# Late attention sums and some turns in two 64-row halves of the array, with four PSUM banks shared and a new order of steps

## The chip, the cores and the metric

The kernel runs on one core of a Trainium2 chip. The metric is the device time of one execution in microseconds (us), before and after one change.

## What is computed

The reference is linear attention followed by a highway layer. For 8 batches (b) and 8 heads, with 576 positions and 64 features a head:

```python
q_s = softmax(q, axis=-1);  k_s = softmax(k, axis=2)      # over features; over positions
kv  = einsum('bhsd,bhse->bhde', k_s, v)                    # 64 x 64 for each head
x   = einsum('bhsd,bhde->bhse', q_s, kv)                   # then 4608 rows of 512
H = max(x @ w_h, 0);  T = sigmoid(x @ w_t + b_t)
out = T * H + (1 - T) * x                                  # 4608 x 512, float32
```

## The kernel before

The 4608 rows are 36 tiles of 128 rows. Tiles 9p to 9p+3 belong to batch 2p, 9p+4 to 9p+7 to batch 2p+1, and 9p+8 takes 64 rows of each ("double tile"). All engines work at once. Their order is written out by hand: `ORDER` is one long list of steps, such as `xu_9_0` or `th_9_0:A`, and each step issues its instructions to its engine in the order of the list. What follows the colon chooses the engine (A ScalarE, D VectorE, P GpSimd) or a form. Every engine works off its own instructions in that order and waits only for data and free buffers. The engines are named as in the profile: PE is TensorE (PEld its weight loads), DVE is VectorE, ACT is ScalarE, POOL is GpSimd, SP is SyncE, which issues nearly all transfers.

The steps of one batch b:

- `k`, `v`, `q` (L180, L193): loads, three landing buffers each, all from SP's queue; the stores `st` (L473) stand in the same queue. For batch 7 `qd` (L337) turns the queries by two DMA transposes, from the same queue.
- `ek`, `eq` (L250, L294): exponentials on ACT. `vc` (L256): cast of v to fp16, by default on POOL.
- `kv` (L262): the products of k and v, 72 matmuls of 64 rows x 64 columns for a batch (two steps of 36 for batches 0 and 1), which use the array in four quarters. `kr` (L278): reciprocal; `kn` (L283): the product with it. `kn` writes the result into `kvb`, a matrix that is zero outside two blocks, so that one matmul over 128 rows makes two heads; it takes two instructions, one for each half of the partitions.
- `qt` (L310): eight (or two) TensorE turns of the query exponentials into the bank `qps`; `qc` (L329) copies them out.

The steps of one tile i:

- `xu` (L348): the sums, four matmuls of 130 columns; 65 columns a head, one of them the sum of the softmax. A double tile has eight, on the two column halves of the array (form `128*64` in the profile). `rs` (L367): reciprocal; `x` (L372): product, both on DVE.
- `xt` (L379): four TensorE turns of x into the bank `turned`; `xe` (L387): copy out, on DVE or ACT.
- `bw` (L394): the bias into a bank `tps`, by a matmul or by an ACT copy (:A). `mt` (L406): four matmuls of 512 columns with w_t onto it. `mh` (L414): four with w_h into a bank `gps`. Tiles 0, 4 and 5 do most steps in two halves.
- `th` (L428): tanh on ACT. `dd` (L437) on DVE. `uu` (L441): the gate, one DVE instruction, or, with :P, two on POOL (a "lifted" gate: L450 and L451). `oo` (L462): the last addition, on POOL. `st`: the store.

`fill` (L165) are matmuls without use before the first loads have landed. The last tile, 35, does its gate in two column halves.

PSUM has eight banks: two for `tps`, two for `gps`, two for the one pair `ps_x` that `kv` and `xu` use in turn, one for `qps`, one for `turned` (L97 to L101, L115).

Of the kernel before, what the change touches and what calls it, by code (L numbers as in the profile page):

```python
# [18 lines left out]
w_t_2 kr_0_0 whd_0:P whd_2:P w_t_0 k_1_2 v_1_2 q_1_0 k_1_0 v_1_0 fill_5 q_1_4 kn_0_0 q_2_0 k_2_0 eq_0_2 xu_0_0 v_2_0  # L19
q_3_0 rs_0_0 whc_0:A x_0_0 k_3_0 fill_4 v_3_0 kv_0_1 fill_3 kr_0_1 kn_0_1 xu_0_1 rs_0_1 xu_1_0 rs_1_0 qt_0_1 x_1_0  # L20
fill_6 whd_3:P qc_0_1 xt_1_0 xu_3_0 qt_0_2 qc_0_2:A xe_1_0:D fill_1 rs_3_0 x_3_0 x_0_1 xt_3_0 xu_2_0 rs_2_0 x_2_0
wtc_2:P whc_2:A mh_1_0 wtc_0:P vc_1_3 ek_1_3 ek_1_2 vc_1_0 xe_3_0:D mh_3_0 dd_1 xt_0_1 xt_0_0 mt_1_0 xe_0_0:D mh_0_0
xe_0_1 dd_3 xt_2_0 mh_0_1 mt_0_1 th_1_0 xe_2_0:D dd_0 vc_1_2:A kv_1_1 uu_1_0 oo_1_0 eq_1_0 mt_0_0 th_0_0 ek_1_0 ek_1_1
kr_1_1 bw_3 qt_1_0 vc_1_1:A kn_1_1 qc_1_0 mt_3_0 xu_5_1 uu_0_0 mh_2_0 th_3_0 bw_2 rs_5_1 x_5_1 dd_2 xu_4_1 kv_1_0
kr_1_0 eq_1_1 rs_4_1 xt_5_1 mt_2_0 th_2_0 kn_1_0 bw_5 xe_5_1:D x_4_1 xu_5_0 mt_5_1 qt_1_1 eq_1_2 rs_5_0 x_5_0 xt_5_0
xu_4_0 bw_4:A uu_3_0:P oo_3_0 xe_5_0:D mh_5_1 rs_4_0 x_4_0 mh_5_0 xt_4_1 qc_1_1:A xt_4_0 xe_4_1:D dd_5 eq_2_0 xe_4_0:D
v_4_0 mt_5_0 th_5_0 xu_6_0 qt_1_2 rs_6_0 qc_1_2 oo_0_0 mt_4_1 mh_4_1 mh_4_0 uu_2_0:P x_6_0 mt_4_0 eq_2_1 xt_6_0 xu_8_0
uu_5_0 bw_6:A xe_6_0:D qt_2_0 rs_8_0 x_8_0 mh_6_0 oo_5_0 th_4_0 xt_8_0 dd_4 uu_4_0 xu_7_0 mt_6_0 ek_2_0:F rs_7_0
vc_2_2:A bw_8 xe_8_0:D mt_8_0 x_7_0 th_6_0 xt_7_0 th_8_0 oo_2_0 vc_2_0 kv_2_0 oo_4_0 qc_2_0 q_4_0 bw_7:A qt_2_1
qc_2_1:A dd_6 uu_6_0:P oo_6_0 eq_3_0:F xe_7_0:D kr_2_0 kn_2_0 mh_8_0 xu_9_0 rs_9_0 x_9_0 mt_7_0 th_7_0 bw_9 dd_8  # L30
uu_8_0:P qt_2_2 qc_2_2:A xu_10_0 bw_10:A xt_9_0 xe_9_0:D rs_10_0 x_10_0 ek_3_0 mh_7_0 dd_7 ek_3_2 mh_9_0 xu_12_0 k_4_0
xt_10_0 k_5_0 rs_12_0 qt_3_0 xe_10_0:D x_12_0 mt_9_0 th_9_0 uu_7_0:P q_4_9 dd_9 xu_11_0 qc_3_0 vc_3_2:A xt_12_0
mt_10_0 rs_11_0 mh_10_0 x_11_0 v_5_0 q_5_0 vc_3_0 st_1_1 q_5_9 uu_9_0 dd_10 oo_7_0 kv_3_0 qt_3_1 th_10_0 oo_8_0 st_1_0
xe_12_0 bw_12:A mh_12_0 kr_3_0 qc_3_1:A kn_3_0 xu_14_0 rs_14_0 x_14_0 bw_11:A xt_11_0 xe_11_0 mt_12_0 th_12_0 qt_3_2
v_6_0 xt_14_0 oo_9_0 k_6_0 xu_13_0 q_6_0 xe_14_0 mh_11_0 dd_12 qc_3_2 mt_11_0 rs_13_0 eq_4_0:F th_11_0 uu_12_0
uu_10_0:P x_13_0 dd_11 xu_15_0 rs_15_0 vc_4_0 mh_14_0 x_15_0 st_5_1 dd_14 qt_4_0 oo_10_0 vc_4_2 xu_16_0 rs_16_0 x_16_0
xt_13_0 xe_13_0:D oo_12_0 bw_14:A bw_13:A ek_4_0:F st_3_0 mt_14_0 th_14_0 xu_17_0 rs_17_0 bw_15:A x_17_0 qc_4_0
xt_15_0 mt_13_0 kv_4_0 xe_15_0:D kr_4_0 uu_11_0:P oo_11_0 th_13_0 qt_4_1 uu_14_0:P st_3_1 mh_13_0 vc_5_2 xt_16_0
kn_4_0 mh_15_0 xe_16_0:D vc_5_0 xu_18_0 ek_5_0:F dd_13 xt_17_0 qc_4_1:A uu_13_0 xe_17_0:D dd_15 rs_18_0 oo_14_0
bw_16:A mt_15_0 mh_16_0 x_18_0 th_15_0 uu_15_0:P mt_16_0 dd_16 mh_17_0 oo_13_0 bw_17:A th_16_0 oo_15_0 kv_5_0 uu_16_0  # L40
kr_5_0 kn_5_0 oo_16_0 eq_4_2 dd_17 qt_4_2 xt_18_0 eq_5_0 mt_17_0 st_5_0 xe_18_0 xu_20_0 rs_20_0 mh_18_0 qc_4_2:A
bw_18:A q_7_0 th_17_0 mt_18_0 eq_5_1 bw_20:A uu_17_0:P x_20_0 xt_20_0 dd_18 vc_6_2 xe_20_0:D xu_21_0 th_18_0 rs_21_0
# [23 lines left out]
def kernel(  # L66
# [40 lines left out]
    b32 = consts.tile([P, DM], FP32, name="b32")  # L107
# [28 lines left out]
    def halves(b, k):  # L136
        return (k, k + 1) if b < 2 else (0, 2)
# [396 lines left out]
```

## Time and profile before

| what | value |
|---|---|
| device time, median of 3 runs | 118.9 us (118.82 to 118.92) |
| the profiled execution, first to last instruction (span) | 116.9 us |
| what lies around the span, by the median | 2.0 us |
| mean granted TensorE clock | 0.995 |
| moved by DMA | 40.58 MB, mean 347 GB/s |
| first matmul of the highway layer (`mh_1`) | 18.14 us |

The profiled execution has no time of its own besides its span; the runs differ among themselves by 0.1 us.

How to read the rows quoted below. A window row gives a stretch, its length, then the busy time of each engine with its count of instructions, the granted clock, the share of the DMA engines and what they moved. A timeline row gives the start, the length, the engine, the line, the operation, what it writes and reads with its shape, and how many instructions are merged in it; brackets tell of idle time before it and what ended it. A matmul's form such as `64*64` is the part of the array that it uses, rows by columns. The length of a matmul holds its way through the array, so neighbours overlap, and the distance from one start to the next is its cost. A group row ends with total busy time, mean ns of one, and idle time before it with its cause.

### The profile page before, as it was taken

The page shows a single profiled execution, that of the slowest core. Times are in us where ns is not written, and L with a number is a line of the kernel's source. Part 1 is how long each engine was busy: PE and PEld are TensorE (multiplying, and loading weights), DVE is VectorE, ACT ScalarE, POOL GpSimd, SP SyncE. Part 2 cuts the span into 40 slices and gives each one's busy share as a digit, 9 for nine tenths or more (in the row PEclk, how much of TensorE's full clock was granted, in tenths as well). Part 3 has the DMA queues.
Part 4 walks back from the last instruction along what each step waited for, and adds up shares of the span by engine and source line. Part 5 has one row for each costly group of instructions (what it writes and reads, how often), then busy time and mean ns, then how long its engine had stood idle before and what let it go on. Part 6 is the DMA issues. An engine that isn't in the chain of part 4 may idle for free.

```text
span 116.9 us, 3424 instructions
## 1 busy us (share of the span) xinstructions
PE 109.5 (94%) x1351; PEld 61.6 (53%) x1351; DVE 93.3 (80%) x222; ACT 90.0 (77%) x132; POOL 89.1 (76%) x99
## 2 busy tenths in 40 slices
PE   5999987999999999999999999999999999999930
PEld 2354544545665656565665547566564555554520
DVE  5642587589799979979889798988989887899870
ACT  4356461897999999989999999998597998545520
POOL 5022237208996999999999999999989699999960
PEclk9999999999999999999999999999999999999998
DMA  2999999999999999999999999999999956992875
GB/s 42 399 392 377 408 398 385 375 377 379 393 391 397 383 391 393 358 375 387 357 376 360 387 392 363 390 381 383 399 398 217 302 204 270 397 404 115 315 295 179
DMA packets 24195, 40.58 MB, mean 347 GB/s; under 512 B 5362, under 2 KB 11762, under 8 KB 24180
## 3 DMA queue, kind: packets, MB, share of 16 engines
q1 hardware_dynamic: 24032, 40.24, 96.9%
q8 instruction: 10, 0.16, 0.6%
q10 hardware_dynamic: 148, 0.14, 0.4%
q14 instruction: 5, 0.04, 0.1%
HBM read 30.41 MB, written 9.44 MB: 341 GB/s over the span
## 4 chain that ended last, share of the span: by engine, by line
PE 67%; POOL 15%; issue 6%; DVE 5%; DMA 3%; SPq 1%; POOLq 0%; DVEq 0%
PE tps L411 18%; PE gps L419 16%; PE turned L167 9%; POOL o L471 7%; PE xu L361 6%; PE turned L384 5%; PE kv L269 5%; PE qps L324 4%; POOL u L451 4%; DMA out_dram<-o 3%; POOL g L450 2%; PE qps L319 2%; POOL v L259 2%; DVE x L376 2%; PE tps L401 1%
## 5 line engine op out<-in xcount | busy, mean ns | idle before, releaser
L471 POOL TENSOR_TENSOR o<-u,x 128x512 f32<-128x512 f16 (+1 forms) x36 | 40.6, 1143 | 1.6 <-DVE u L453 0.7
L411 PE MATMUL tps<-w16t,xT 128*128 128x512 f16 (+1 forms) x148 | 37.3, 373 | 0.0
L419 PE MATMUL gps<-w16h,xT 128*128 128x512 f16 x144 | 36.8, 379 | 0.5 <-DVE xT L391 0.5
L376 DVE TENSOR_TENSOR x<-xu,rs 128x512 f16<-128x512 f32 (+1 forms) x39 | 25.2, 649 | 2.4
L259 POOL CAST v<-v 128x1152 f16<-128x1152 f32 (+1 forms) x14 | 14.0, 1010 | 14.7 <-DMA v<-in_v_dram 13.7
L439 DVE SCALAR_TENSOR_TENSOR d<-x,gps 128x512 f16<-128x512 f16 x36 | 24.5, 680 | 0.3
L451 POOL TENSOR_TENSOR u<-g,d 128x512 f16<-128x512 f16 x17 | 19.7, 1158 | 1.7 <-DVE rs L370 0.4
L253 ACT ACTIVATE ek<-k 128x576 f16<-128x576 f32 (+2 forms) x15 | 17.9, 1225 | 3.0 <-DMA k<-in_k_dram 3.0
L419 PEld LDWEIGHTS <-xT 128*128 128x128 f16 x144 | 13.0, 98 | 12.3 <-DVE xT L391 1.8
L399 ACT COPY tps<-ball 128x512 f32<-128x512 f32 x28 | 16.6, 597 | 3.5 <-DVE u L453 3.2
L411 PEld LDWEIGHTS <-xT 128*128 128x128 f16 x148 | 13.2, 98 | 10.6 <-DVE xT L391 0.4
L361 PE MATMUL xu<-kvb,eq 128*128 128x130 f16 (+1 forms) x160 | 14.8, 224 | 0.2 <-DVE kvb L287 0.2
L384 PE MATMUL turned<-idh,x 128*128 128x128 f16 x144 | 14.2, 220 | 0.5 <-DVE x L376 0.5
L391 DVE COPY xT<-turned 128x512 f16<-128x512 f16 (+1 forms) x28 | 10.9, 391 | 4.2 <-PE turned L384 3.0
L435 ACT ACTIVATE tps<-tps 128x512 f32<-128x512 f32 (+1 forms) x20 | 11.2, 559 | 3.6 <-PE tps L411 3.3
L453 DVE SCALAR_TENSOR_TENSOR u<-tps,d 128x512 f16<-128x512 f32 (+1 forms) x19 | 12.7, 671 | 1.4 <-ACT tps L435 0.6
L361 PEld LDWEIGHTS <-eq 128*128 128x128 f16 (+1 forms) x160 | 10.0, 100 | 7.3 <-DVE x L376 2.5
L167 PE MATMUL turned<-blank 128*128 128x512 f16 x40 | 12.4, 458 | 1.5 <-POOL blank L149 1.3
L384 PEld LDWEIGHTS <-x 128*128 128x128 f16 x144 | 9.8, 98 | 6.0 <-DVE x L376 2.1
L307 ACT ACTIVATE qe<-q 128x1024 f16<-128x1024 f32 (+3 forms) x9 | 9.4, 1052 | 4.1 <-DMA q<-in_q_dram 4.1
L450 POOL TENSOR_SCALAR g<-th 128x512 f16<-128x512 f16 x17 | 10.6, 621 | 0.9 <-ACT th L433 0.9
L433 ACT ACTIVATE th<-tps 128x512 f16<-128x512 f32 x17 | 10.0, 594 | 0.9 <-PE tps L411 0.9
(48 smaller groups left out, 106.8 us busy)
## 6 DMA issues: line engine op xcount, KB each, us to landing
k<-in_k_dram SPq DMA_DIRECT2D x6, 1152.0 KB, 12.2
v<-in_v_dram SPq DMA_DIRECT2D x6, 1152.0 KB, 12.0
out_dram<-o SPq DMA_DIRECT2D x23, 256.0 KB, 4.0
q<-in_q_dram SPq DMA_DIRECT2D x10, 512.0 KB, 11.5
out_dram<-o SPq DMA_DIRECT2D x6, 512.0 KB, 3.8
k<-in_k_dram SPq DMA_DIRECT2D x4, 576.0 KB, 9.3
q<-in_q_dram SPq DMA_DIRECT2D x2, 1152.0 KB, 14.2
q<-in_q_dram SPq DMA_DIRECT2D x2, 640.0 KB, 10.5
```

What stands on the lines that cost most here:

```text
L167: nc.tensor.matmul(spare, blank[:, 0:P], blank, start=True, stop=True, skip_group_check=True)
L253: nc.scalar.activation(t[:, :, c:c + n].rearrange("p j c d -> p c j d"), T[f"k32{b}"][:, c:c + n].rearrange("p c (j d) -> p c j d", j=NJ), ...
L259: copy(v16[b % NV][:, c:c + n, :, 0:D], T[f"v32{b}"][:, c:c + n].rearrange("p c (j d) -> p c j d", j=NJ))
L361: nc.tensor.matmul(dst, turned_q(b, jp, n), kvb[b % NKV][:, hh, kk], start=True, stop=True, skip_group_check=True)
L376: nc.vector.tensor_mul(t[:, k0:k1], sums(i, k)[:, :, :, 0:64], T[f"rs{i}_{k}"][:, 0:k1 - k0].unsqueeze(3).to_broadcast([P, k1 - k0, 4, D]))
L384: nc.tensor.matmul(t[:, n], T[f"x{i}"][:, n0 + n % 2:n0 + 2 * P:2], idh, is_transpose=True, start=True, stop=True, skip_group_check=True)
L399: nc.scalar.copy(t[:, cs], ball[:, cs])
L411: nc.tensor.matmul(T[gate(i, k)][:, cs], T[f"xT{i}"][:, n], w16["t"][:, n, cs], start=False, stop=(n == parts[-1] and not first), skip_gro ...
L419: nc.tensor.matmul(t, T[f"xT{i}"][:, n], w16["h"][:, n], start=(first and n == parts[0]), stop=(n == parts[-1] and not (first and len(part ...
L439: nc.vector.scalar_tensor_tensor(t, T[f"x{i}"], -0.5, T[f"gps{i}"], op0=ALU.mult, op1=ALU.max)
L451: nc.gpsimd.tensor_mul(t, g, T[f"d{i}"])
L471: eng.tensor_add(t[:, cs], T[f"u{i}_{h}"][:, cs], T[f"x{i}"][:, cs])
```

## The change

1. **Sums from tile 9 on in halves of 64 rows.** A new matrix `kvl` holds the key-value product of both heads without zeros, with ones at its edges (`setuplate`, three small POOL memsets early on). `xu` issues eight matmuls of 64 rows and 65 columns in place of four of 128 rows and 130 columns; the two halves write two banks. Double tiles 17, 26 and 35 issue sixteen, in quarters.
2. **The key-value norm of batches 2 to 7 in one instruction**, since `kvl` has no blocks to keep apart.
3. **Turns in halves.** From tile 9 and batch 3 on, a turn that is not marked `:W` in the list is made of 64-row halves into two banks, twice as many matmuls of 64 columns. These are `xt` of tiles 17, 20, 21, 24, 25, 26, 28, 29, 31, 32, 33 and 34 and `qt` 5_0, 6_0 and 6_1; the other 25 late turns are marked `:W`. `xe` and `qc` read the two banks in one instruction.
4. **Four banks given out one by one.** The pair `ps_x` and the banks `qps` and `turned` become two pairs, `ps_s`; `pair_user` and the loop behind it go through the list and give each use a pair, or a bank to a turn marked `:W`. Early turns and fills share one pair.
5. **The bias on DVE** (`bw:D`) is a new choice.
6. **A new list** with the same steps and `setuplate`. Counts of what changes its engine:

| step | before | after |
|---|---|---|
| `bw` | 9 PE, 28 ACT | 5 PE, 22 ACT, 10 DVE (2, 3, 7, 10, 15, 18, 23, 24, 25, 28) |
| `uu`, by tile | 19 DVE, 17 POOL | 15 DVE, 21 POOL |
| `vc`, batches 2 to 7 | 10 POOL, 2 ACT | 6 POOL, 6 ACT |
| `vc`, batches 0 and 1 | 4 POOL, 3 ACT, 1 DVE | 3 POOL, 4 ACT, 1 DVE |
| `qc`, wide (g 0 and 1) | 8 DVE, 6 ACT | 12 DVE, 2 ACT |
| `qc`, narrow (g 2) | 2 DVE, 6 ACT | 6 DVE, 2 ACT |
| `xe` | 28 DVE, 11 ACT | 27 DVE, 12 ACT |
| `wtc` | 2 POOL | 1 POOL, 1 ACT |

The TensorE steps of the new list from the first late sum on; a bar stands where the division of the array changes (52 here, 13 ahead of it). In the old list it changes only into and out of its ten `kv` steps and its four double sums, which all stand alone (28).

```
xu_11 xu_10 | mt_6 mt_4_1 mt_4 xt_10 qt_3_1 mh_4_1 xt_11 mh_10 | xu_9 xu_12 | mt_11 mt_10 qt_3_0 qt_3_2 xt_9 mh_11
xt_12 | kv_3 | mt_9 | xu_13 xu_14 | mh_9 mh_12 xt_14 mt_12 | xu_16 xu_15 | mh_14 mt_14 xt_13 xt_16 qt_4_1 mh_13 xt_15
mt_13 qt_4_0 mh_16 | kv_4 xu_17 | mt_15 mt_16 | xu_21 xt_17 | mh_15 | qt_5_0 xt_21 | mt_17 | xu_20 xu_18 | mh_17 mh_21
mt_21 | xt_20 | kv_5 | xu_19 | mh_20 qt_4_2 xt_18 mt_20 xt_19 qt_5_1 mt_18 | xu_23 xu_24 | mh_19 mh_18 | xu_22 xt_24 |
mt_19 xt_23 qt_5_2 mt_24 xt_22 | xu_26 | mh_24 mt_23 | qt_6_0 xu_25 | mh_22 mt_22 | xt_26 xt_25 | mh_23 | qt_6_1 | kv_6 |
mh_25 | xu_27 xu_29 | mh_26 mt_25 xt_27 mt_26 | xu_28 xt_29 | mh_27 mh_29 | kv_7 | xt_28 | mt_27 | xu_33 xu_32 | mh_28
mt_28 | xt_32 xt_33 | mt_29 | xu_34 xu_31 | mh_33 mh_32 mt_32 | xt_31 xu_30 | mt_33 qt_6_2 qt_7_2 mh_31 xt_30 mt_31 |
xu_35 | xt_34 | mt_30 mh_30 mh_34 xt_35 mt_34 bw_35_1 bw_35_0 mh_35 mt_35 mt_35_1
```

SP's queue around the last loads, before: `q_7_0 st_7_0 v_7_0 st_7_1 st_10_1 k_7_0 st_10_0 qd_7_0 q_7_9 qd_7_1`; after: `q_7_0 st_7_0 k_7_0 v_7_0 st_12_0 st_16_0 st_10_0 qd_7_0 qd_7_1`. Nine stores stand ahead of the last large load in both.

The core of the diff (the lists are left out):

```diff
-    ps_x = pool("ps_x", 1, space=PS)
-    ps_q = pool("ps_q", 1, space=PS)
-    ps_xt = pool("ps_xt", 1, space=PS)
+    ps_s = pool("ps_s", 1, space=PS)
...
+    EARLY, EARLY_Q = 9, 3
...
+    banks = [ps_s.tile([P, 2, DM], FP32, tag=f"s{i}", name=f"space{i}") for i in range(2)]
+    space, held = {}, [None] * 4
+    for now, (u, s) in enumerate(zip(users, ORDER.split())):
+        if u and u not in space:
+            last = [-1 if h is None else final[h] for h in held]
+            if s.endswith(":W"):
+                n = min((n for n in range(4) if last[n] < now), key=lambda n: (last[n ^ 1] < now, last[n]))
+                space[u], held[n] = banks[n // 2][:, n % 2:n % 2 + 1], u
+            else:
+                n = min((n for n in (0, 2) if max(last[n:n + 2]) < now), key=lambda n: max(last[n:n + 2]))
+                space[u], held[n:n + 2] = banks[n // 2], [u, u]
...
     def kn(e, b, k):
         k0, k1 = halves(b, k)
+        if b >= 2:
+            nc.vector.tensor_mul(kvl[b % NKV][:, :, :, 1:65], kv_of(b, k)[:, :, :, 0:64],
+                                 T[f"rz{b}_{k}"].unsqueeze(3).to_broadcast([P, 2, 2, 64]))
+            return
...
     def xu(e, i, k):
...
+        if i >= EARLY:
+            for n in range(4):
+                kk, hh = n // 2, n % 2
+                for a, b in enumerate(bs):
+                    for w in range(2):
+                        part = slice(64 * w, 64 * w + 64)
+                        rows = slice(0, P) if len(bs) == 1 else slice(64 * a, 64 * a + 64)
+                        nc.tensor.matmul(t[rows, w, 65 * n:65 * n + 65], turned_q(b, jp, n)[part],
+                                         kvl[b % NKV][part, hh, kk, hh:hh + 65],
+                                         start=True, stop=True, skip_group_check=True)
+            return
...
     def xt(e, i, k):
         k0, k1 = heads(i, k)
-        t = T[f"xtps{i}"] = turned[:, 0]
+        if in_rows("xt", i, k):
+            t = T[f"xtps{i}"] = space[f"xt{i}"].bitcast(FP16)
+            for n in range(4):
+                n0 = n // 2 * 2 * P
+                for r in range(2):
+                    rows = slice(64 * r, 64 * r + 64)
+                    nc.tensor.matmul(t[:, r, 64 * n:64 * n + 64], T[f"x{i}"][rows, n0 + n % 2:n0 + 2 * P:2],
+                                     idh[rows, rows], is_transpose=True, start=True, stop=True,
+                                     skip_group_check=True)
+            return
...
         if e == "A":
             nc.scalar.copy(t[:, cs], ball[:, cs])
+        elif e == "D":
+            nc.vector.tensor_copy(t[:, cs], ball[:, cs])
```

`qt_rows` does for the query turns what `xt` does here, with eight pairs of matmuls (two for g 2); `rs` and `x` read the sums in their new places with one instruction each, as before.

More of the change, by code (lines that the diff above doesn't have):

```diff
@@ L112 @@
     NKV, NV = 3, 2
-    kvb = [consts.tile([P, 2, 2, 130], FP16, name=f"kvb{i}") for i in range(NKV)]
+    kvb = [consts.tile([P, 2, 2, 130], FP16, name=f"kvb{i}") for i in range(2)]
+    kvl = [consts.tile([P, 2, 2, 66], FP16, name=f"kvl{i}") for i in range(NKV)]
     v16 = [consts.tile([P, 4, NJ, 66], FP16, name=f"v16_{i}") for i in range(NV)]
-    turned = ps_xt.tile([P, 2, 4, P], FP16, tag="xtps", name="turned")
-    spare = turned.rearrange("p a c d -> p (a c d)").bitcast(FP32)
     T = {}
@@ L157, in setup_dve @@
         nc.vector.memset(ones[32:33], 1.0)
-        for i in range(NKV):
+        for i in range(2):
             nc.vector.memset(kvb[i], 0.0)
@@ L312, in qt @@
         a, s = (2, 2) if g < 2 else (1, 1)
-        t = T[f"qps{b}_{g}"] = ps_q.tile([P, a, 4, s * NP], FP16, tag="qps", name=f"qps_{b}_{g}")
+        if in_rows("qt", b, g):
+            qt_rows(b, g)
+            return
+        room = space["early" if b < EARLY_Q else f"qt{b}_{g}"][:, 0].bitcast(FP16)
+        t = T[f"qps{b}_{g}"] = room[:, 0:a * 4 * s * NP].rearrange("p (a n t) -> p a n t", a=a, n=4)
         if b in WIDE and g < 2:
```

173 lines of the change are left out of this document (121 added, 52 removed).

## The prediction

> **What bounds the kernel now.** I read the page first, for the shares and the chain, then the windows by stage, then TensorE's timeline around the steps that change, then the groups by shape. The page:
>
> ```profile
> span 116.9 us, 3424 instructions
> PE 109.5 (94%) x1351; PEld 61.6 (53%) x1351; DVE 93.3 (80%) x222; ACT 90.0 (77%) x132; POOL 89.1 (76%) x99
> DMA  2999999999999999999999999999999956992875
> PE 67%; POOL 15%; issue 6%; DVE 5%; DMA 3%; SPq 1%; POOLq 0%; DVEq 0%
> ```
>
> Everything looks full: TensorE (PE) holds two thirds of the chain, but the transfers are busy to the 32nd of 40 slices and GpSimd (POOL) holds 15%. The windows tell where each engine has room:
>
> ```profile
> core 0: us, PE busy (x) PEld busy (x) DVE busy (x) ACT busy (x) POOL busy (x), PEclk, DMA share, GB/s
> 20.00:40.00 20.00, 20.00 (x290) 11.26 (x288) 16.70 (x45) 18.11 (x26) 12.91 (x15) 1.00 1.06 384
> 40.00:60.00 20.00, 19.99 (x307) 12.10 (x305) 17.70 (x40) 19.41 (x26) 19.41 (x20) 1.00 1.06 378
> 60.00:80.00 20.00, 20.00 (x287) 11.67 (x285) 17.43 (x39) 19.15 (x28) 19.61 (x20) 1.00 1.07 378
> 80.00:93.00 13.00, 12.99 (x133) 7.48 (x135) 12.12 (x26) 10.59 (x15) 11.54 (x13) 1.00 1.13 341
> 93.00:112.00 19.00, 19.00 (x206) 10.68 (x193) 16.22 (x34) 12.62 (x26) 17.46 (x18) 1.00 0.76 290
> ```
>
> From 20 to 112 us TensorE never pauses and its clock is full (1.00). VectorE (DVE) works 80.2 of these 92 us (the five added, 87%), ScalarE (ACT) 79.9, GpSimd 80.9, and GpSimd's missing time is nearly all before 40 us. A busy TensorE could still be a slow one, so I read the starts:
>
> ```profile
> 61.90 0.38 PE L419 MATMUL gps<-w16h,xT 128*128 128x512 f16 x1
> 62.11 0.40 PE L361 MATMUL xu<-kvb,eq 128*128 128x130 f16 x4
> 62.35 0.39 PE L384 MATMUL turned<-idh,x 128*128 128x128 f16 x4
> 62.57 0.38 PE L411 MATMUL tps<-w16t,xT 128*128 128x512 f16 x1
> ```
>
> The durations overlap; the distance from start to start is what a step costs. A matmul over 512 columns takes 0.21 us (61.90 to 62.11), the four of a tile's sums 0.23 (0.24 here, four columns' worth of 0.21 x 130/512 = 0.053 plus a few ns each), the four turns 0.22. That is 0.42 ns a column with next to nothing between. So TensorE's work is the first bound, and a change that shortens it gains only as long as VectorE, GpSimd and the loads keep up.
>
> **The change: TensorE.** Two steps of the old list already use a divided array, and they carry the prices. Tile 8's sums, in two 64-column halves:
>
> ```profile
> 34.04 0.39 PE L384 MATMUL turned<-idh,x 128*128 128x128 f16 x4
> 34.36 0.42 PE L361 MATMUL xu<-kvb,eq 128*64 128x130 f16 x8
> 34.72 0.62 PE L324 MATMUL qps<-idh,qe 128*128 128x128 f16 x8
> 35.17 1.03 PE L419 MATMUL gps<-w16h,xT 128*128 128x512 f16 x4
> ```
>
> The four turns need 0.22 us, but the sums begin 0.32 after them: going into the divided array costs 0.10. The eight sums and the way back take 0.36; with 0.10 for the way back, eight matmuls of 130 columns took 0.26, or 0.065 for two, against 0.057 for one undivided. So two halves do run beside each other. A key-value step in four quarters:
>
> ```profile
> 48.62 0.78 PE L269 MATMUL kv<-v,ek 64*64 64x65 f16 x72
> 49.33 0.62 PE L324 MATMUL qps<-idh,qe 128*128 128x128 f16 x8
> ```
>
> It takes 0.71 us, less 0.10 for the way back 0.61: 8.5 ns a matmul, 34 ns for four side by side, where 65 columns alone would be 27. The new steps are halves by rows (64 rows, all 128 columns), which no row shows. Bounds for one side-by-side pair of 64 or 65 columns: 27 ns from below (columns alone), 57 from above (an undivided sum, if the 128-column weights cannot be loaded faster than in the undivided steps). I take 34, the nearest row in columns. The weight loads argue for it:
>
> ```profile
> L384 PEld LDWEIGHTS <-x 128*128 128x128 f16 x144 | 9.8, 98 | 6.0 <-DVE x L376 2.1
> L269 PEld LDWEIGHTS <-ek 64*64 64x64 f16 x576 | 5.5, 106 | 3.4 <-issue 0.8 <-ACT v L259 0.8 <-ACT ek L253 0.5
> L361 PEld LDWEIGHTS <-eq 128*64 128x64 f16 x32 | 1.0, 109 | 1.5 <-DVE x L376 1.0 <-issue 0.4
> ```
>
> A load of 128 columns (98 ns, mostly latency) is no longer than one of 64 columns (106 to 109).
>
> Now the sum. 24 single tiles (9 to 34 without 17 and 26) go from 0.23 to four pairs, 0.136: 24 x 0.094 = 2.3 us. The three double tiles (17, 26, 35) go from 0.26 to 16 quarters at 8.5 ns, 0.136: 0.4. Twelve tile turns go from 0.22 to 0.136: 1.0. Three query turns (5_0, 6_0, 6_1) go from 0.45 to eight pairs, 0.27: 0.5. Four biases (2, 3, 8, 9) leave TensorE for DVE and ACT: 4 x 0.21 = 0.9. Saved: 5.1 us. Against it stand the changes of division. The old list has 28 (ten key-value steps and four double sums, in and out). In the new list, step by step, I count 65, five of them between quarters and halves. 37 more at 0.098 are 3.6 us. **TensorE net: -1.5 us**; with 27 ns a pair -2.6, with 57 ns +2.3; if the five inner changes are free, another -0.5. Break-even is where the 168 pairs cost 9 ns more: 43 ns a pair.
>
> **VectorE.**
>
> ```profile
> L333 DVE COPY eq<-qps 128x1024 f16<-128x1024 f16 x8 | 5.5, 684 | 1.6 <-PE qps L324 1.6
> L333 DVE COPY eq<-qps 128x256 f16<-128x256 f16 x2 | 0.5, 262 | 0.0
> L287 DVE TENSOR_TENSOR kvb<-kv,rz 64x256 f16<-64x256 f32 x12 | 5.1, 424 | 0.3
> L453 DVE SCALAR_TENSOR_TENSOR u<-tps,d 128x512 f16<-128x512 f32 x18 | 12.3, 685 | 1.3 <-ACT tps L435 0.6
> L391 DVE COPY xT<-turned 128x512 f16<-128x512 f16 x23 | 9.5, 413 | 2.7 <-PE turned L384 1.5 <-ACT tps L435 0.7
> ```
>
> It gains ten bias copies. No row has a 512-wide fp32 copy on DVE: below it is the fp16 copy, 0.41, above the fp32 three-operand one, 0.685; I take 0.65, near the fp32 row: +6.5 (4.1 to 6.9). It gains four wide and four narrow query copies from ACT: 4 x 0.684 + 4 x 0.262 = +3.8. It loses four gates (u) to GpSimd, -2.7; one key-value norm in each of six batches, -2.5; one turn copy, -0.4. Net +4.7; neighbours overlap by some 0.08 and there are seven more of them, so about **+4.1 us** (1.7 to 4.5) on top of 80.2. A bias copy waits on DVE until the tanh or gate before it has read its bank; behind it in DVE's queue stand other tiles' reciprocals and products, for which TensorE's turns wait.
>
> **GpSimd, ScalarE, loads.**
>
> ```profile
> L450 POOL TENSOR_SCALAR g<-th 128x512 f16<-128x512 f16 x17 | 10.6, 621 | 0.9 <-ACT th L433 0.9
> L451 POOL TENSOR_TENSOR u<-g,d 128x512 f16<-128x512 f16 x17 | 19.7, 1158 | 1.7 <-DVE rs L370 0.4
> L259 POOL CAST v<-v 128x1152 f16<-128x1152 f32 x10 | 11.3, 1147 | 1.0 <-PE tps L411 0.9
> L399 ACT COPY tps<-ball 128x512 f32<-128x512 f32 x28 | 16.6, 597 | 3.5 <-DVE u L453 3.2
> L333 ACT COPY eq<-qps 128x1024 f16<-128x1024 f16 x6 | 6.1, 1009 | 0.4 <-PE qps L324 0.3
> 21.89 0.59 ACT L435 ACTIVATE tps<-tps 128x512 f32<-128x512 f32 x1
> 27.19 1.16 POOL L471 TENSOR_TENSOR o<-u,x 128x512 f32<-128x512 f16 x1
> ```
>
> GpSimd takes four more gates (0.62 + 1.16 each, +7.1) and gives up four wide casts (-4.6): +2.5. But tile 1's gate is now its own and can start when the tanh of 21.89 ends, near 22.5, where GpSimd's run of tiles now begins at 27.19. It starts 4.7 earlier with 2.5 more to do: -2.2, no bound. The early memsets and the weight cast that leaves it lie in its idle time before that. ScalarE sheds six biases (-3.6) and four wide query copies (-4.0) and takes four wide casts, priced by GpSimd's 1.147 (+4.6): about -3, no bound.
>
> ```profile
> 77.69 0.59 SPq L183 DMA_DIRECT2D k<-in_k_dram  x1
> k<-in_k_dram SPq DMA_DIRECT2D x6, 1152.0 KB, 12.2
> 90.11 2.12 ACT L253 ACTIVATE ek<-k 128x2304 f16<-128x2304 f32 x1
> 92.80 0.78 PE L269 MATMUL kv<-v,ek 64*64 64x65 f16 x72
> ```
>
> The last large load, the keys of batch 7, is issued at 77.69 and by the median lands near 89.9; its exponential runs at 90.11 and batch 7's key-value step at 92.80. The new list has the same loads and again nine stores ahead of the last one, so with full queues it lands at the same time; but the last one is now v, which needs two casts of 1.15 side by side in place of 2.12. Key-value step 7 may come near 91.3, 1.5 earlier, and the TensorE steps behind it sum to 0.9 less. The loads allow -2.4, more than TensorE can give.
>
> In the new list sums often come in twos, so each turn waits for a reciprocal and a product on DVE behind another tile's; what is queued behind is the next mh and mt, and with a full TensorE every such wait adds to the end. The old list had few such waits. I give 0.4 us for new ones: **-1.5 + 0.4 = -1.1 us**, span 115.8. The span of before leaves 2.0 us to the median of 118.9 (116.9 + 2.0), which I carry over: **117.8 us**.
>
> **The rivals.** (a) A larger gain: the inner changes are free, a pair costs 27 to 30 ns, no new waits. -2.0 to -2.6: 116.6. For it: DVE and GpSimd have ends that allow it if packed densely; against it, packing is already dense. (b) The gain is taken by the others: DVE or the last load sets the end, 118.9. For it: transfers are full to slice 32, and the two DMA turns of batch 7's queries now stand behind both last loads and three stores. (c) DVE becomes the bound, between 30 and 80 us where most of the new copies lie. It needs 80.2 + 4.1 = 84.3 us. At its mean density of 87% that is 96.7 us in place of 92, +4.7; at the 93% of its densest stage (12.12 of 13) 90.6, -1.4. The even point is 84.3/92 = 91.6%. Halfway between, 90%, gives 93.7: +1.7, 120.6. For it: no earlier stage passed 89%; against it: TensorE, not DVE, set the pace there, and the bias copy may cost 0.41 only. (d) The halves do not gain what they should: the pairs cost 57 ns (weights not loaded in time, or the halves run one after the other). This is the one mechanism that loses on TensorE itself, in every late sum, from 43 ns a pair on: +2.3, and 121.6 with the same 0.4 of waits. For it: no row shows 128-column weights under fewer than 128 columns; against it: the two rows of divided steps. A milder form is a floor in time from one matmul's start to the next, whatever its width: two halves then cost twice the floor. The 72 key-value matmuls in 0.61 us, 8.5 ns apart, leave it little, so I give it 0.03 of (d)'s chance. The Trainium skill states such a floor, "TensorE: Matmul & The Clock Gate", section "Wait — 56ns, not 53.3ns?": start-to-start is never below about 25 ns however small the matmul is. By it a pair would cost 50 ns and the change of TensorE's work would be +1.2 us instead of -1.5, 120.5 with the same waits; this trace's 8.5 ns speaks against it.
>
> **How the numbers follow.** Forecast, 116.9 to 118.5: 0.41. (a): 0.08. (b), 118.5 to 119.3: 0.16, a quarter of it still faster, half the same. (c), 119.3 to 121: 0.21. (d): 0.14. A measurement of this kernel tells about 0.2% from no change. Faster 0.41 + 0.08 + 0.04 = 0.53, same 0.08, slower 0.04 + 0.21 + 0.14 = 0.39. The range leaves out the lower part of (a) and nearly all of (d), under 2 in 10: 116.4 to 120.8. Cases of both signs hold most of the chance; the likeliest alone is 116.9 to 118.5.
>
> **What would show it.** The starts of a late pair of sums: two tiles in about 0.27 us plus 0.10 at each end, right; 0.45 plus the ends, (d). A DVE bias copy near 0.65, and DVE above 91% from 30 to 93 us with TensorE waiting for products or turn copies, (c). GpSimd's first gate near 22.5. Key-value step 7 before 92 us and TensorE's last matmul near 110.5. What would make the prediction wrong: a price of a change between halves and quarters well over 0.10, slower copies out of the two half-row banks, or a bank that is freed late, all of which would appear as gaps between TensorE's steps.

## The result, and the profile after

The kernel after takes 123.1 us (122.7 and 123.5; two more executions, 125.0 and 125.5 us at a lower clock, are left out), against 118.9 us before: ratio 1.036, 95% interval 1.032 to 1.039. It is slower by 4.2 us, where the forecast was 1.1 us faster with a range up to 120.8. The profiled execution is the one of 122.7 us. Its page:

```profile
span 120.8 us, 3808 instructions
...
PE 107.0 (89%) x1539; PEld 57.5 (48%) x1539; DVE 95.3 (79%) x226; ACT 89.4 (74%) x125; POOL 90.0 (75%) x104
...
DMA  3999999999999999999999999999999811989284
...
PE 56%; DMA 22%; DVE 12%; ACT 4%; issue 2%; SPq 1%; DVEq 0%
```

TensorE's busy time fell from 109.5 to 107.0 us, yet the span grew by 3.9. No engine is fuller than before; TensorE holds less of the chain, VectorE more (12% after 5%). So it is waiting, not work. DMA's 22% of the chain are loads of the first 28.6 us, the longest one of batch 1's queries (13.4 us); the chain of own_banks, an experiment below that takes 119.0 us, holds them too, so they do not make the difference. The windows tell where TensorE waits:

```profile
core 0: us, PE busy (x) PEld busy (x) DVE busy (x) ACT busy (x) POOL busy (x), PEclk, DMA share, GB/s
20.00:40.00 20.00, 18.14 (x204) 10.25 (x203) 15.97 (x41) 17.14 (x25) 14.49 (x16) 1.00 1.06 386
40.00:60.00 20.00, 18.46 (x317) 10.58 (x314) 17.55 (x41) 16.80 (x23) 16.58 (x17) 1.00 1.07 378
60.00:80.00 20.00, 19.09 (x351) 10.66 (x350) 16.97 (x38) 16.81 (x24) 18.42 (x20) 1.00 1.06 388
80.00:93.00 13.00, 12.55 (x227) 6.59 (x226) 12.23 (x26) 12.26 (x17) 11.54 (x13) 1.00 1.02 314
93.00:112.00 19.00, 19.00 (x265) 9.23 (x264) 17.77 (x41) 13.55 (x23) 18.43 (x19) 1.00 0.69 256
```

TensorE, which was never idle before from 20 us on, now lacks 1.86, 1.54, 0.91 and 0.45 us in the first four windows. VectorE is no fuller in them: 62.7 of 73 us, against 64.0 in the same four windows before. A first pause stands ahead of the windows; the timeline of the kernel after from 14 us (query turns `qt_0_1` end at 14.2; then come six fills, and the copy of the query turns):

```profile
14.20 1.46 PE L201 MATMUL space<-blank 128*128 128x512 f16 x6
...
15.70 0.69 DVE L400 COPY eq<-space 128x1024 f16<-128x1024 f16 x1 [0.81 <-PE space L201]
...
16.44 0.38 PE L491 MATMUL space<-idh,x 128*128 128x128 f16 x4 [0.78 <-DVE eq L400]
...
17.21 0.37 ACT L400 COPY eq<-space 128x256 f16<-128x256 f16 x1 [1.30 <-PE space L389]
...
17.61 0.42 DVE L502 COPY xT<-space 128x512 f16<-128x512 f16 x1 [1.22 <-ACT eq L400]
```

Read the brackets. The copy out of the query turns' bank was held by L201, the fills, which write the *other* bank. Tile 1's turn (16.44) writes the fills' bank and waited for the copy of the query bank. The copy of that turn (17.61) waited for an ACT copy of the query bank. None of these pairs touches the same bank. What they share is a tile: the new kernel declares two banks as one lasting tile (`banks[i]`, L170), and a step on a part of it is ordered after the steps on the other part. The same later, with two turns marked `:W`, each in a bank of its own (`qt_3_0` and `qt_3_2`):

```profile
49.78 0.61 PE L389 MATMUL space<-idh,qe 128*128 128x128 f16 x8
...
50.19 0.68 DVE L554 SCALAR_TENSOR_TENSOR d<-x,gps 128x512 f16<-128x512 f16 x1
...
50.79 0.68 DVE L400 COPY eq<-space 128x1024 f16<-128x1024 f16 x1
...
51.53 0.27 PE L389 MATMUL space<-idh,qe 128*128 128x128 f16 x2 [1.13 <-DVE eq L400]
```

The second turn needs nothing of the copy at 50.79, and TensorE stands still from the end of the first to 51.53.

To compare kernels I add up TensorE's pauses from the starts of its matmuls: of each distance from one start to the next I take away what the first matmul needs (0.42 ns a column and 2.5 ns, or up to 60 ns for one on a divided array, and 97 ns for a change of division); what remains over 15 ns is a pause, all else is work. All numbers are in us; the times are medians, the rest is from the profiled executions:

| kernel | time | work | pauses to 20 us | 20 to 34 | after 34 | last matmul starts |
|---|---|---|---|---|---|---|
| before | 118.9 | 104.5 | 4.6 | 0.5 | 1.0 | 111.8 |
| after | 123.1 | 102.7 | 5.2 | 2.9 | 3.7 | 115.7 |
| own_banks | 119.0 | 102.8 | 3.8 | 2.8 | 1.4 | 112.1 |
| own_early | 121.4 | 102.8 | 4.3 | 2.8 | 3.5 | 114.7 |
| own_late | 121.7 | 102.8 | 5.9 | 3.8 | 1.6 | 115.4 |
| own_whole_turns | 118.7 | 103.5 | 3.7 | 2.8 | 0.1 | 111.4 |
| own_whole_both | 121.0 | 103.5 | 4.2 | 2.7 | 2.2 | 113.9 |
| old_list_halves | 120.6 | 106.6 | 4.5 | 0.5 | 0.6 | 113.4 |
| before_one_tile | 134.7 | 104.3 | 5.9 | 2.0 | 14.8 | 128.4 |

From before to after, TensorE's work fell by 1.8 us and its pauses rose by 5.7: together the 3.9 of the span.

A part of the first column of pauses is not waiting. In every trace the first fills start 0.43 us apart in place of 0.21, and the count takes the excess for pauses. This lasts until 6.4 us in the kernel before (2.6 us of excess), 3.9 in the kernel after (1.4) and 4.3 in own_banks (1.5). The change does not set it, for own_early and own_late, whose first steps are those of own_banks, have slow fills until 6.4 us. Without this excess, the pauses rose by 6.9 us from before to after.

### The profile page after: what moved, and what is told of

It is laid out like the page before. It is cut to its first block, busy times and chain, and to the rows that moved or that the text cites. A ratio compares the mean times of both kernels' runs of the same rounds, so it can differ in the third digit from the quotient of the medians.

```text
span 120.8 us, 3808 instructions
## 1 busy us (share of the span) xinstructions
PE 107.0 (89%) x1539; PEld 57.5 (48%) x1539; DVE 95.3 (79%) x226; ACT 89.4 (74%) x125; POOL 90.0 (75%) x104
## 4 chain that ended last, share of the span: by engine, by line
PE 56%; DMA 22%; DVE 12%; ACT 4%; issue 2%; SPq 1%; DVEq 0%
PE gps L534 21%; PE tps L526 19%; DMA q<-in_q_dram 14%; DMA w32h<-in_moe_w_h_dram 8%; PE space L491 4%; PE space L436 4%; PE space L303 3%; DVE x L467 3%; DVE eq L400 2%; DVE d L554 2%; PE space L389 2%; PE space L483 2%; DVE xT L502 1%; ACT eq L400 1%; DVE tps L514 1%
## 5 line engine op out<-in xcount | busy, mean ns | idle before, releaser
L566 POOL TENSOR_TENSOR u<-g,d 128x512 f16<-128x512 f16 x21 | 24.3, 1155 | 3.0 <-DVE rs L458 0.8
L467 DVE TENSOR_TENSOR x<-space,rs 128x512 f16<-128x512 f32 x27 | 18.1, 688 | 1.2
L293 POOL CAST v<-v 128x1152 f16<-128x1152 f32 (+1 forms) x9 | 8.8, 987 | 8.6 <-DMA v<-in_v_dram 8.6
L512 ACT COPY tps<-ball 128x512 f32<-128x512 f32 x22 | 13.0, 592 | 1.4 <-DVE u L568 1.1
L201 PE MATMUL space<-blank 128*128 128x512 f16 x40 | 11.1, 421 | 2.6 <-POOL blank L146 1.3
L491 PE MATMUL space<-idh,x 128*128 128x128 f16 x96 | 9.6, 219 | 3.2 <-DVE eq L400 1.2
L400 DVE COPY eq<-space 128x1024 f16<-128x1024 f16 (+1 forms) x16 | 8.6, 536 | 4.8 <-PE space L201 3.3
L568 DVE SCALAR_TENSOR_TENSOR u<-tps,d 128x512 f16<-128x512 f32 (+1 forms) x15 | 9.9, 663 | 1.1 <-ACT tps L550 0.8
L502 DVE COPY xT<-space 128x512 f16<-128x512 f16 (+1 forms) x18 | 6.8, 388 | 4.2 <-ACT eq L400 1.2
L293 ACT CAST v<-v 128x1152 f16<-128x1152 f32 (+1 forms) x10 | 9.5, 955 | 0.2 <-DMA v<-in_v_dram 0.2
```

The costliest lines, as they stand in the source:

```text
L293: copy(v16[b % NV][:, c:c + n, :, 0:D], T[f"v32{b}"][:, c:c + n].rearrange("p c (j d) -> p c j d", j=NJ))
L467: nc.vector.tensor_mul(t.rearrange("p k (w h) e -> p w k h e", w=2), pairs(i)[:, :, :, 1:129].rearrange("p w k (h e) -> p w k h e", h=2), ...
L491: nc.tensor.matmul(t[:, n], T[f"x{i}"][:, n0 + n % 2:n0 + 2 * P:2], idh, is_transpose=True, start=True, stop=True, skip_group_check=True)
L512: nc.scalar.copy(t[:, cs], ball[:, cs])
L566: nc.gpsimd.tensor_mul(t, g, T[f"d{i}"])
```

## The experiments

**Theory one:** the pauses come from banks that share a tile. **Theory two:** they come from VectorE, which has more to do (the forecast's rival c).

### own_banks: each use of a bank gets a tile of its own

List, instructions and banks are those of the kernel after; only the declaration changes.

```diff
-    banks = [ps_s.tile([P, 2, DM], FP32, tag=f"s{i}", name=f"space{i}") for i in range(2)]
...
+        if u == "early":
+            space[u] = [region(r, 2).tile([P, DM], FP32, tag=f"h{h}", name=f"early{h}") for h in range(2)]
+        elif half is None:
+            space[u] = region(r, 1).tile([P, 2, DM], FP32, tag="pair", name=f"space_{u}")
+        else:
+            space[u] = region(r, 2).tile([P, DM], FP32, tag=f"h{half}", name=f"space_{u}").unsqueeze(1)
```

> The kernel after with the same list, the same banks and the same instructions, but each single bank (early turns and fills, late turns marked :W) is a tile of its own instead of a half of a lasting two-bank tile. Theory one, waits across the banks of one tile: the copy of a turn out of one bank no longer waits for a fill or turn in the other; TensorE's first useful highway matmul comes back from 19.4 to about 18.2 us, and some 4 us of its later pauses go: about 118 us (117.3 to 118.8) against 123.1 after. Theory two, VectorE is the bound: its work is unchanged, so it stays at 122 or more.

Measured: 119.0 us, ratio to before 1.000 (0.998 to 1.002). 4.1 us are back with the same work on every engine, as theory one has it. Theory two falls: VectorE is busy 95.1 us here and 95.3 in the kernel after. The early stretch, for comparison with the rows above:

```profile
14.11 1.46 PE L219 MATMUL early<-blank 128*128 128x512 f16 x6
14.40 0.68 DVE L418 COPY eq<-early 128x1024 f16<-128x1024 f16 x1
...
15.40 0.39 PE L509 MATMUL early<-idh,x 128*128 128x128 f16 x4
...
15.83 0.42 DVE L520 COPY xT<-early 128x512 f16<-128x512 f16 x1 [0.75 <-PE early L509]
```

The copy runs beside the fills, 1.3 us earlier, and each wait is for the step that made the data. But the 1.1 us that were forecast did not come either. The pairs, too, are declared anew for each use here; that it is the sharing that costs is read from the waits between banks above and tested by before_one_tile below.

### own_early and own_late: a part of the banks each

`own_early` gives own tiles to the early turns and fills alone, `own_late` to all later uses alone.

```diff
 # own_late, against own_banks
-            space[u] = [region(r, 2).tile([P, DM], FP32, tag=f"h{h}", name=f"early{h}") for h in range(2)]
+            shared = region(r, 1).tile([P, 2, DM], FP32, tag="pair", name="early")
+            space[u] = [shared[:, 0], shared[:, 1]]
 # own_early, against own_banks
-        elif half is None:
-            space[u] = region(r, 1).tile([P, 2, DM], FP32, tag="pair", name=f"space_{u}")
...
+        if r not in lasting:
+            lasting[r] = region(r, 1).tile([P, 2, DM], FP32, tag="pair", name=f"space{r}")
+        space[u] = lasting[r] if half is None else lasting[r][:, half:half + 1]
```

> As own_banks, but only the early turns and fills get banks of their own; late turns marked :W stay halves of lasting two-bank tiles. Theory one: the early part of the loss comes back, 1.3 us before the first highway matmul and about 1.2 us of pauses up to 36 us: about 120.5 us. Theory two: 122 or more, as the early stage is not where VectorE is full.

> The kernel after; only what uses the banks after the early part (sums, key-value steps, turns from tile 9 and batch 3 on) gets its own tile each time, the two early banks stay one lasting tile. The complement of own_early, which won back 1.7 of the 4.1 us that own_banks wins. Theory one, with costs that add: 119.0 + 1.7 = 120.7 us (120.2 to 121.2). If the early waits are made up for later, so that only the late ones count: about 119.0.

Measured: own_early 121.4 us, ratio 1.020 (1.017 to 1.023); own_late ratio 1.023 (1.017 to 1.029), 121.7 us against its own 118.98, with executions from 121.2 to 123.2. Both came out 0.9 to 1 us above what was expected of them. Alone they win back about 1.7 and 1.4 us, together 4.1, so both stretches cost. That this is more than the sum is in part the clock: in own_late's profiled execution (122.4 us) TensorE ran at half its clock from 20.1 to 23.5 us, which costs 1.7 of its 3.8 us between 20 and 34 (by the count above). Its window:

```profile
20.00:23.50 3.50, 3.50 (x16) 1.58 (x14) 1.19 (x3) 1.05 (x2) 0.00 (x0) 0.51 1.07 374
```

The trace of own_early has no such stretch after its first fills. The executions of own_late scatter too much to say whether the rest adds up.

### before_one_tile: the same wait alone, in the old kernel

The kernel before, with list, instructions and banks unchanged; the bank of the query turns and that of the tile turns become one tile.

```diff
-    turned = ps_xt.tile([P, 2, 4, P], FP16, tag="xtps", name="turned")
+    both = ps_s.tile([P, 2, DM], FP32, tag="both", name="both")
+    turned = both[:, 1].bitcast(FP16).rearrange("p (a c d) -> p a c d", a=2, c=4)
...
-        t = T[f"qps{b}_{g}"] = ps_q.tile([P, a, 4, s * NP], FP16, tag="qps", name=f"qps_{b}_{g}")
+        room = both[:, 0].bitcast(FP16)
+        t = T[f"qps{b}_{g}"] = room[:, 0:a * 4 * s * NP].rearrange("p (a n t) -> p a n t", a=a, n=4)
```

> The kernel before with its list, its instructions and its banks; only the bank of the query turns and the bank of the tile turns are declared as one lasting tile of two banks. Theory one (steps on one bank of a tile wait for steps on its other bank): slower than 118.9 us by over 1.5 us, 120.5 to 123, with TensorE's turns and their copies waiting for each other where the kernel before does not wait. Theory two (how the banks are declared costs nothing, and what own_banks won came from something else): 118.6 to 119.3.

Measured: 134.7 us, ratio 1.129 (1.124 to 1.135). The direction is theory one's, but the size is nearly four times the most that I allowed (4.1): 15.7 us for one declaration. TensorE's work is what it was (104.3 us); its pauses grew from 6.0 to 22.7. Some 1.6 us of this growth are again matmuls at half the clock, from 19.9 to 23.3 us; the rest is waiting. One of the waits in its timeline:

```profile
45.28 1.01 ACT L334 COPY eq<-both 128x1024 f16<-128x1024 f16 x1 [0.47 <-PE both L325]
...
46.33 0.43 DVE L392 COPY xT<-both 128x512 f16<-128x512 f16 x1 [1.15 <-ACT eq L334]
46.56 1.16 POOL L474 TENSOR_TENSOR o<-u,x 128x512 f32<-128x512 f16 x1
46.67 0.17 DVE L281 RECIPROCAL rz<-kv 128x4 f32<-128x4 f32 x1
46.87 0.86 DVE L287 TENSOR_TENSOR kvb<-kv,rz 64x256 f16<-64x256 f32 x2
...
47.79 0.41 PE L362 MATMUL xu<-kvb,eq 128*128 128x130 f16 x4 [1.68 <-DVE kvb L287]
```

This shows why so small a wait grows. VectorE's turn copy stands behind an ACT copy of the other bank (1.15 us). VectorE works in order, so batch 2's reciprocal and norm stand behind the turn copy, and the sums, which wait for the norm, hold TensorE for 1.68 us. The row at 47.79 blames the norm; the cause stands at 46.33.

### bias_act: the ten VectorE biases on ScalarE

The kernel after, with `:A` in place of `:D` in all ten places:

```diff
-... bw_3:D ... bw_2:D ... bw_7:D ... bw_10:D ... bw_15:D ...
+... bw_3:A ... bw_2:A ... bw_7:A ... bw_10:A ... bw_15:A ...
```

> The kernel after, with its ten bias copies of VectorE given to ScalarE at the same places of the list. Theory two, VectorE is the bound: 6.5 us less work on it, so 2 us or more faster than after, 121 or less. Theory one: the pauses stay, within 0.7 us of after, 122.4 to 123.8, or a little slower where ScalarE stands in the way.

Measured: 130.5 us, ratio 1.095 (1.090 to 1.099): neither. At these places of the list ScalarE has no room:

```profile
27.04 1.25 ACT L287 ACTIVATE ek<-k 128x576 f16<-128x576 f32 x2
...
28.20 0.58 ACT L512 COPY tps<-ball 128x512 f32<-128x512 f32 x1
28.71 0.68 ACT L287 ACTIVATE ek<-k 128x576 f16<-128x576 f32 x1
29.29 0.66 ACT L293 CAST v<-v 128x576 f16<-128x576 f32 x1
29.85 0.58 ACT L512 COPY tps<-ball 128x512 f32<-128x512 f32 x1
30.48 1.44 PE L526 MATMUL tps<-w16t,xT 128*128 128x512 f16 x3 [3.76 <-ACT tps L512]
```

Two biases stand behind batch 1's exponentials and casts, and TensorE waits 3.76 us for the second. The run says nothing on theory two, which own_banks decides.

### old_list_halves: the divided sums alone, in the old list

The kernel before with the late sums in halves and the norm of batches 2 to 7 in one instruction; list (with `setuplate`) and banks are the old ones.

```diff
+        if i >= EARLY:
+            for n in range(4):
...
+                        nc.tensor.matmul(t[rows, w, 65 * n:65 * n + 65], turned_q(b, jp, n)[part],
+                                         kvl[b % NKV][part, hh, kk, hh:hh + 65],
+                                         start=True, stop=True, skip_group_check=True)
+            return
```

> The kernel before with its own list and its own banks, only with the sums of tiles 9 to 35 in 64-row halves and the key-value norm of batches 2 to 7 in one instruction. In the old list each late sum stands alone, so each pays two changes of division. By the prices of the prediction TensorE saves 2.3 us on single tiles and 0.4 on double ones and pays 24 x 2 x 0.098 = 4.7 us: +2.0, about 120.9 us. If a change of division cost nothing in place, 116.2; if the halves did not run side by side, 123 or more.

Measured: 120.6 us, ratio 1.014 (1.010 to 1.017). TensorE's work rose by 2.1 us: by the forecast's prices 48 more changes of division at 0.098 cost 4.7 and the sums give back 2.7, 2.0 in all. The prices hold in sum.

### own_whole_turns: the fifteen late turns undivided

Own banks, the list of the kernel after, but no turn is made of halves.

```diff
     def in_rows(kind, i, g):
-        return i >= (EARLY if kind == "xt" else EARLY_Q) and f"{kind}_{i}_{g}" not in WHOLE
+        return False
```

> own_banks with the fifteen late turns that are divided made whole, in the same list and banks. Priced by the start distances of the traces TensorE's work is 0.75 us more (1.73 us of turns more, ten changes of division less at 0.098). Theory (after the early part TensorE's own work sets the time, one for one): 119.0 + 0.75 = 119.75 us (119.4 to 120.1). Rival (another engine or the loads set it): 118.8 to 119.2.

Measured: 118.7 us, ratio to before 0.997 (0.995 to 0.9985): 0.3 us faster than own_banks where it should have been 0.75 slower, and the only version faster than both kernels; its interval just excludes no change. TensorE's work rose by 0.74 us as priced, but 1.3 us of pauses after 34 us went. In own_banks, two pauses stand within rows of short matmuls that wait for nothing visible; the first, on TensorE's timeline:

```profile
66.38 0.38 PE L544 MATMUL tps<-w16t,xT 128*128 128x512 f16 x1
66.69 0.20 PE L454 MATMUL space_xu<-kvl,eq 64*128 64x65 f16 x1
67.42 0.27 PE L454 MATMUL space_xu<-kvl,eq 64*128 64x65 f16 x6 [0.53 <-issue]
```

The pauses are 0.67 and 0.50 us, and each ends 1.4 us after a 16 KB packet of the instruction queue has passed (66.0 and 87.5 us). The program of own_banks needs twelve such packets, of own_whole_turns eleven, of before ten. That points to TensorE's supply of instructions; it was not shown. Against a mere count of packets stands the kernel after, with twelve and no such pause; for the supply speaks spliced36 (below), where 0.68 us without a visible cause end at 72.8 us, 1.3 us after a packet. Without these pauses TensorE is full in own_whole_turns after 34 us:

```profile
core 0: us, PE busy (x) PEld busy (x) DVE busy (x) ACT busy (x) POOL busy (x), PEclk, DMA share, GB/s
20.00:34.00 14.00, 12.42 (x156) 6.83 (x156) 10.71 (x30) 12.26 (x20) 9.39 (x11) 1.00 1.06 383
34.00:60.00 26.00, 26.00 (x385) 15.37 (x384) 24.66 (x55) 24.56 (x30) 24.73 (x26) 1.00 1.06 381
60.00:80.00 20.00, 20.00 (x352) 11.34 (x350) 18.25 (x41) 18.08 (x27) 19.01 (x20) 1.00 1.06 389
```

### own_whole_both: the sums undivided too

own_whole_turns, with the late sums of the kernel before and the norm in two instructions. The same `if` goes in `xu`, `rs` and `x`, and the third `kvb` is back in place of `kvl`.

```diff
     def kn(e, b, k):
         k0, k1 = halves(b, k)
-        if b >= 2:
-            nc.vector.tensor_mul(kvl[b % NKV][:, :, :, 1:65], kv_of(b, k)[:, :, :, 0:64],
-                                 T[f"rz{b}_{k}"].unsqueeze(3).to_broadcast([P, 2, 2, 64]))
-            return
...
     def xu(e, i, k):
-        if i >= EARLY:
+        if False:
```

> own_whole_turns with the late sums made whole as well (and the key-value norm in two steps again), so that no step is divided but the key-value steps and the double tiles, as in the kernel before; list, banks and DVE biases are those of own_whole_turns. Priced by start distances, 108 undivided sums cost 2.82 us more and 28 fewer changes of division give 2.74 back: +0.08 us on TensorE, and 2.5 us more on VectorE. If TensorE alone sets the time: 118.7 to 118.9 us. If VectorE has no room: 119.3 to 121. If the divided sums are worth what the forecast gave them (2.3 us before the changes of division): 120 or more.

Measured: 121.0 us, ratio 1.016 (1.013 to 1.019). TensorE's work is the same to 0.03 us, as priced, but VectorE's is 2.9 us more (98.2), and TensorE's pauses after 34 us grow from 0.1 to 2.2. They stand mostly where sums wait for the norm. First the norm's groups, of own_whole_turns:

```profile
L338 DVE TENSOR_TENSOR kvl<-space_kv,rz 128x256 f16<-128x256 f32 x6 | 2.6, 427 | 0.2
```

and of own_whole_both, with one of the places in its timeline:

```profile
L339 DVE TENSOR_TENSOR kvb<-space_kv,rz 64x256 f16<-64x256 f32 x12 | 5.1, 421 | 0.3
```

```profile
41.10 0.86 DVE L339 TENSOR_TENSOR kvb<-space_kv,rz 64x256 f16<-64x256 f32 x2
...
42.02 0.71 PE L459 MATMUL space_xu<-kvb,eq 128*128 128x130 f16 x8 [0.22 <-DVE kvb L339]
```

So in this list the divided sums earn nothing on TensorE. They earn 2.3 us, most of it because `kvl` lets the norm be one instruction: at five places TensorE waits 0.26 to 0.39 us for the norm, 1.8 us in all; the second instruction takes 0.42 each time. Whether a VectorE without room or the longer norm alone makes these waits, the run does not separate.

### spliced36 and reordered_whole: the stage from 20 to 34 us

own_banks and own_whole_turns pause 2.8 us there, the kernel before 0.5. One pause of own_whole_turns there, 0.8 us up to 28.66, waits for exponentials of batch 1's queries, whose load ScalarE has waited for until 28.19. In the kernel before, ScalarE waits for these queries until 28.26, but TensorE has other steps in the meantime. Two other orders were tried, by list alone. spliced36 is own_banks with the first 201 steps in the old order, then tile 6's tanh and maximum, then the rest in the new order:

```diff
+... (the old list up to) xu_7_0 mt_6_0 th_6_0 dd_6 setuplate bw_8:A q_4_0 oo_2_0 xe_8_0:D mt_8_0 rs_7_0 mh_8_0 ...
```

reordered_whole is own_whole_turns with one stretch rewritten:

```diff
-... eq_1_2 kv_1_1 kr_1_1 kn_1_1 eq_1_1 bw_8:A mt_3_0 kv_1_0 kr_1_0 xu_5_1 q_4_0 qt_1_2 kn_1_0 xu_5_0 qc_1_2 th_3_0 ...
+... kv_1_1 kr_1_1 kn_1_1 mt_3_0 xu_5_1 xu_4_1 rs_5_1 x_5_1 th_3_0 eq_1_2 eq_1_1 kv_1_0 kr_1_0 xt_5_1 xe_5_1:D kn_1_0 bw_5 mt_5_1 ...
```

> own_banks with another list: the first 201 steps in the order of the kernel before (to about 36 us), then what is left in the order of the kernel after. In own_banks TensorE stands 2.8 us between 20 and 34 us, waiting for the loads and casts of batch 1, and 0.5 us there in the kernel before. Theory (what is left of the lost gain is the new order in this stage): 119.0 - 2.3 + 0.7 for the early lead that goes + 0.4 for two biases that are matmuls again = 117.8 us (117.3 to 118.3), better than both kernels. Rival (the end is held by something later, the loads or VectorE): 118.7 to 119.5.

> own_whole_turns with one stretch of its list rewritten (from the exponentials of batch 1's queries to tile 5's sums): the first halves of tiles 5's and 4's sums, tile 5's first turn and its first highway product come before the step that waits for the query load, and tile 3's tanh comes before the two exponentials that wait for that load. In own_whole_turns TensorE stands 2.76 us between 20 and 34 us, and nowhere after. Theory (what is left of the lost gain is the order of this stage, and TensorE bounds the rest): about 1.2 us of these pauses go, 118.7 - 1.2 = 117.5 us (117.0 to 118.0). Rival (the loads of batch 1 hold the stage whatever the order, or another engine is the bound after it): 118.4 to 119.0.

Measured: spliced36 124.4 us, ratio 1.043 (1.039 to 1.047). The stage's pauses fell to 0.4 us, but 6.7 us stand between 34 and 60, all before 52 us and most of them just behind the seam. Its timeline there:

```profile
36.59 1.02 PE L544 MATMUL tps<-w16t,xT 128*128 128x512 f16 x4
...
37.65 0.58 ACT L568 ACTIVATE tps<-tps 128x512 f32<-128x512 f32 x1 [2.10 <-PE tps L544]
...
38.15 0.58 ACT L530 COPY tps<-ball 128x512 f32<-128x512 f32 x1
...
38.78 1.02 PE L544 MATMUL tps<-w16t,xT 128*128 128x512 f16 x4 [1.17 <-ACT tps L530]
```

The next bias stands behind tile 6's tanh, and the list gives TensorE nothing else. Behind these waits, 1.5 of the 6.7 us are matmuls at half the clock, from 48.0 to 51.4 us. The run decides nothing. reordered_whole takes 119.25 us, ratio 1.001 (0.999 to 1.004), a little over the rival's bounds: 2.7 of the 2.8 us are still there, at other steps. The order that I tried did not help; what would have is open.

## Why the prediction was wrong, point by point

- **The step that failed** is "I give 0.4 us for new ones", the new waits. The pauses rose by 5.7 us (6.9 without the slow first fills). With own banks 3.8 of them go, and 4.1 us of the time: waits between the banks of one tile. The forecast went through the list for what each step needs, and never asked what the new declaration of the banks makes it wait for, though `banks[i]` stands in the diff. It named "a bank that is freed late" only as something that could go wrong, at no price. The rest, 2.0 us net, is what own_banks has over before: 2.3 more between 20 and 34 us, for which the new list is the likely cause (no order that was tried removed them without losing elsewhere), and 1.2 without a visible cause, against 0.8 fewer later and 0.7 fewer before 20 us. These 0.7 are no merit of the list, as own_banks' fills came to the full clock 2.1 us sooner. All this eats the whole gain of TensorE, so that own_banks ends at the time of before. That lies in the range of rival (b), but not for its reason: in own_banks TensorE is full after 34 us but for those two pauses and 0.13 us more, so neither the loads nor VectorE set its end.
- **TensorE's work, -1.5 us,** was right: -1.8. The prices held too. Two tiles' sums on TensorE's timeline of the kernel after:

```profile
53.82 1.04 PE L526 MATMUL tps<-w16t,xT 128*128 128x512 f16 x4
54.79 0.42 PE L436 MATMUL space<-kvl,eq 64*128 64x65 f16 x16
55.14 0.60 PE L534 MATMUL gps<-w16h,xT 128*128 128x512 f16 x2
```

  Four matmuls of 0.21 us end near 54.69, so going in costs 0.10; the sixteen and the way out take 0.35, that is 32 ns a pair (34 forecast). Changes between halves and quarters are not free: 95 to 98 ns like the others. Rival (d) is refuted, its milder form too: in the trace the two matmuls of a pair start 3 to 4 ns apart, so a pair does not pay a floor twice. The floor of about 25 ns from start to start that the Trainium skill states ("TensorE: Matmul & The Clock Gate", "Wait — 56ns, not 53.3ns?") does not hold between the two halves: the sixteen start 16 ns apart on average. On the same half they start 29 to 39 ns apart, which does not speak against it.
- **VectorE:** the bias copy takes 0.687 us, the upper end (0.65 taken):

```profile
L514 DVE COPY tps<-ball 128x512 f32<-128x512 f32 x10 | 6.9, 687 | 0.1
```

  Its busy time rose by 2.0 us, not 4.1. The prices were right, for the durations added up rose by 4.4 us (+4.7 forecast); what was too small is the overlap of neighbours, 2.4 us in place of 0.6. Rival (c) did not happen, since own_banks does the same VectorE work 4.1 us sooner. But own_whole_both, with 2.9 us more on VectorE, loses 2.3; that may be the bound that (c) described, or the longer norm alone.
- **The divided steps** brought little by the forecast's own prices. own_whole_both, the new list undivided, has 0.7 us more of TensorE's work than own_banks; the four biases taken off TensorE are 0.9 of the 1.8. The forecast set -5.1 against +3.6 and did not ask which edit earned the rest.
- **What was to show it:** key-value step 7 came at 97.8 us (forecast before 92), GpSimd's first gate at 23.1 (22.5), the last matmul at 115.7 (110.5). The sign "gaps between TensorE's steps" was the right one.

## What to carry to other kernels

When buffers are merged, ask first what the waits are attached to: put each bank that is used by itself into a tile of its own, or steps on one bank wait for steps on the other. Where a bracket in the timeline names a releaser that touches other data than the waiting step, the declaration is the suspect, and an engine that works in order multiplies the wait. And price each edit by itself: here the division of the turns won nothing, and the divided sums paid through the shorter norm on VectorE.

## What the runs showed of the hardware

A pause can cost more than its length, because TensorE's granted clock may fall. In bias_act it was 0.50 from 28.8 us, within the pause of 3.8 us, to 35.6 us (the windows of that kernel, behind the counts of POOL; the first holds most of the pause):

```profile
26.00:30.40 4.40, 0.73 (x4) 0.21 (x3) 1.28 (x2) 4.40 (x8) 2.19 (x3) 0.82 1.06 390
30.40:35.20 4.80, 4.72 (x52) 2.34 (x51) 1.41 (x4) 2.37 (x5) 1.97 (x3) 0.50 1.06 392
```

Its matmuls of 512 columns start 0.43 us apart there, in place of 0.21. Shorter pauses came before such a stretch as well. The early waits between banks make three pauses of 0.9, 1.1 and 0.6 us between 15 and 20 us. With them the clock fell to half for 3.4 us in own_late (from 20.1 us), before_one_tile (19.9) and bias_act (18.6), but it stayed at 1.00 in the profiled execution of the kernel after, which has the same three. In spliced36 it fell, from 48.0 us, with pauses of 0.9 to 1.7 us; later pauses of 1.8 us in before_one_tile left it at 1.00. No profile without such pauses shows a lower clock between the first fills and the last matmuls. That pauses cause it fits all these traces; what decides whether they do is not shown.
